# Two turned pairs of attention in one visit of TensorE

## The chip, the cores and the metric

The kernel runs on one core of one Trainium2 chip. The metric is the device time of one execution in microseconds (us); lower is better. An engine is named as in the profile: PE is TensorE, DVE VectorE, ACT ScalarE, POOL GpSimd, SP the queue that issues most DMAs.

## What is computed

A causal attention with a decay over 8 batches and 8 heads (576 positions, 64 channels a head), and on its output a two-layer network with a leaky activation:

```python
scores = scale * np.matmul(q, k.transpose(0, 1, 3, 2))
cum = np.cumsum(np.log(np.clip(f, 0.0001, 1.0)), axis=-1)
scores = np.where(causal, -1000000000.0, scores + cum[:, :, :, None] - cum[:, :, None, :])
attn = np.exp(scores - np.max(scores, axis=-1, keepdims=True))
attn = attn / (np.sum(attn, axis=-1, keepdims=True) + 1e-09)
x = np.matmul(attn, v)              # heads side by side: 4608 tokens x 512
h = x @ w_in                        # 512 -> 2048
g = np.maximum(h, 0.0) + alpha * np.minimum(h, 0.0)
return g @ w_out                    # 2048 -> 512
```

## The kernel before

**Stages.** Two heads make a pair; there are 32 pairs, four to a batch. PE starts on attention, and as soon as the four pairs of a batch have their output, the first layer of the network for that batch can run on it (line 381 with `xx,wi`: 1728 matmuls of 512 columns, twelve to a group that fills one bank of PSUM; the helper `mm` at line 381 issues nearly all matmuls). Attention and first layer share PE until pair 31 is done; then come the rest of the first layer and the second layer (`wot`, `gh`).

**Who sets the order.** The program records operations with a planner (`Plan`), which puts each engine's instructions into a fixed order at build time. It takes on each engine the operation that can begin soonest by its own estimate of durations, and among those the lowest key; a table `SHIFT` adds an offset to the keys by kind of operation and by number. `glue=1.5` lets an operation keep its place at the head though it must wait up to 1.5 us. On the chip each engine then runs its list strictly in order and waits by semaphores.

**A turned pair.** From pair 8 on (`turned`) a pair goes this way:

1. *Tail*: the last 64 queries of both heads, full-array matmuls into two banks (`tail`), small and free to stand anywhere before its pair.
2. *Scores*: twenty matmuls on halves of the rows of the array (64x128 in the profile), two at a time into two banks, six banks in all (`visit`: tiles 0 and 1 share two banks, tile 2 has two, tile 3 has two).
3. DVE reads each bank once (`red`, line 830 for the tiles, 680 for the tail), adds the decay and takes the minimum, and writes into the one buffer `bE`; a bank is free when DVE has read it. ACT takes the exponential in place (line 637).
4. When all nine exponentials are there, DVE turns `bE` in four pieces into four buffers `bm` (line 846, `TK`). `bE` is then free for the next pair.
5. Sixteen DMAs (line 854) gather the pieces into one of two buffers `bTT`: even pairs into the one called `big` in the names, odd pairs into `wr`. Ten are issued by SP, six by POOL.
6. *Values*: sixty matmuls on halves of the columns (128x64) from `bTT` into two banks, which ACT empties (line 925). `bTT` is then free.

So PE meets three layouts of its array: full (first layer, tails), half rows (scores), half columns (values).

**A visit.** `attention(n)` makes one visit for pair n: the values of pair n-2 first, then the scores of pair n. The values carry the requirement that six banks of `rS` are free, and the three groups of scores are glued behind:

```python
after = behind.pop(0) if len(behind) > 1 else None
a = op("PE", ns_v + 400, vp, st, rdy + vd, vb, need=(rS, len(vb[:2]) + 4))
s = op("PE", ..., lambda part=part: rows_of_scores(part), -3000, got, bS[g] + held, glue=1.5)
```

Between two visits stand about four groups of the first layer and one tail. A planned idle time of PE of over half a microsecond in the first 82 us is filled with dummy matmuls (`fill`, line 479), which compute nothing.

Of the kernel before, what the change touches and what calls it, by code (L numbers as in the profile page):

```python
# [18 lines left out]
NP = H // 2  # L19
# [11 lines left out]
NV2 = 6  # L31
# [23 lines left out]
SHIFT = {('L', 0): 9.4, ('D', 0): 2.2, ('Z', 0): 60.6, ('A', 0): 2.2, ('T', 0): -0.3, ('V', 0): -13.3, ('Q', 0): 36.2, ('X', 0): -10.8, ('L', 1): 26.8, ('D', 1): 1.4, ('Z', 1): -27.5, ('A', 1): 47.1, ('T', 1): 17.0, ('V', 1): 48.8, ('X', 1): 122.0, ('L', 2): 28.7, ('D', 2): 45.5, ('Z', 2): 10.6, ('A', 2): 54.0, ('T', 2): 1.8, ('V', 2): 58.1, ('Q', 2): -44.8, ('X', 2): 24.9, ('L', 3): 15.8, ('D', 3): -69.7, ('Z', 3): 0.9, ('A', 3): 165.1, ('T', 3): -84.7, ('Q', 3): 0.7, ('D', 4): -10.7, ('Z', 4): 63.2, ('A', 4): 13.0, ('T', 4): 4.2, ('V', 3): 35.9, ('Q', 4): 132.1, ('X', 3): -15.3, ('L', 5): 81.7, ('D', 5): -4.2, ('Z', 5): -0.4, ('A', 5): 21.2, ('T', 5): -65.7, ('V', 4): 1.3, ('Q', 5): -3.4, ('X', 4): 18.4, ('L', 6): 69.8, ('D', 6): 30.4, ('A', 6): 173.3, ('T', 6): 64.2, ('V', 5): 16.9, ('L', 7): 15.0, ('D', 7): -6.8, ('Z', 7): -95.9, ('A', 7): 218.4, ('T', 7): 47.3, ('V', 6): -17.7, ('V', 7): -37.7, ('Q', 7): -7.0, ('X', 5): -14.8, ('X', 6): -7.2, ('W', 0): 14.3, ('W', 1): 178.8, ('W', 2): 130.1, ('W', 3): -7.0, ('W', 4): 29.0, ('W', 5): 13.1, ('W', 6): 131.9, ('W', 7): -0.1, ('W', 8): -24.7, ('W', 9): 48.7, ('W', 10): -21.0, ('W', 11): -226.7, ('W', 12): -27.8, ('W', 13): 9.3, ('W', 14): 110.8, ('W', 15): 19.8, ('L', 8): -132.0, ('D', 8): -70.2, ('Z', 8): -11.8, ('S', 8): 10.0, ('A', 8): 59.0, ('L', 9): 6.4, ('D', 9): -6.1, ('Z', 9): 32.3, ('S', 9): -81.3, ('A', 9): -1.9, ('Q', 9): -96.4, ('X', 7): 3.1, ('L', 10): 50.1, ('Z', 10): 7.2, ('S', 10): 75.8, ('A', 10): -14.4, ('V', 8): -29.5, ('L', 11): 6.9, ('Z', 11): 41.4, ('S', 11): -6.8, ('A', 11): -68.7, ('V', 9): 12.9, ('Q', 11): 10.9, ('X', 8): 37.3, ('X', 9): 119.6, ('L', 12): 6.3, ('Z', 12): -18.6, ('S', 12): 23.7, ('A', 12): -9.9, ('V', 10): -2.9, ('L', 13): 2.6, ('Z', 13): -3.7, ('S', 13): 27.4, ('A', 13): 27.1, ('V', 11): -0.8, ('Q', 13): -134.7, ('X', 10): 5.7, ('X', 11): 5.8, ('L', 14): 1.6, ('Z', 14): 459.3, ('S', 14): -32.6, ('A', 14): -10.4, ('V', 12): 1.0, ('L', 15): 34.3, ('Z', 15): 17.4, ('S', 15): 96.4, ('A', 15): -40.5, ('V', 13): -69.9, ('Q', 15): -38.3, ('X', 13): 4.3, ('L', 16): 2.7, ('Z', 16): -198.9, ('S', 16): -187.7, ('A', 16): 154.9, ('V', 14): -18.6, ('L', 17): -9.2, ('Z', 17): 0.6, ('S', 17): 49.4, ('A', 17): -109.5, ('Q', 17): -229.2, ('X', 14): 26.2, ('X', 15): -29.2, ('L', 18): -40.0, ('Z', 18): -30.3, ('S', 18): 19.5, ('A', 18): -44.4, ('V', 16): 8.7, ('L', 19): -4.1, ('Z', 19): 16.8, ('S', 19): -29.0, ('A', 19): -99.9, ('V', 17): -19.8, ('Q', 19): -113.9, ('X', 16): 4.8, ('X', 17): -2.5, ('L', 20): -18.2, ('Z', 20): -4.1, ('S', 20): 3.5, ('A', 20): -15.6, ('V', 18): -13.2, ('L', 21): 24.2, ('Z', 21): -5.1, ('S', 21): 30.9, ('A', 21): 1.5, ('V', 19): -12.3, ('Q', 21): -6.5, ('X', 18): -66.7, ('X', 19): 21.5, ('L', 22): -197.2, ('Z', 22): -25.6, ('S', 22): -118.4, ('A', 22): 52.2, ('V', 20): 46.3, ('L', 23): 3.6, ('Z', 23): 49.0, ('S', 23): 3.0, ('A', 23): -4.3, ('V', 21): 106.1, ('Q', 23): -43.7, ('X', 20): 27.7, ('X', 21): -18.4, ('L', 24): -6.9, ('Z', 24): 91.0, ('S', 24): 17.4, ('A', 24): 103.3, ('V', 22): -23.4, ('L', 25): -7.9, ('Z', 25): 14.7, ('S', 25): -51.9, ('A', 25): 20.7, ('V', 23): 21.8, ('Q', 25): 14.2, ('X', 22): 35.9, ('X', 23): -3.3, ('L', 26): -42.8, ('Z', 26): 29.2, ('S', 26): 11.4, ('A', 26): 78.5, ('V', 24): 156.6, ('L', 27): -38.3, ('Z', 27): 1.9, ('S', 27): 40.9, ('A', 27): 0.5, ('Q', 27): 2.0, ('X', 24): -6.8, ('X', 25): 12.5, ('L', 28): -1.5, ('Z', 28): -21.7, ('S', 28): 28.1, ('A', 28): -23.8, ('V', 26): 13.8, ('L', 29): 6.3, ('Z', 29): -5.4, ('S', 29): -109.1, ('A', 29): -4.1, ('V', 27): -32.8, ('Q', 29): -0.6, ('X', 26): -3.0, ('X', 27): -14.3, ('L', 30): -20.4, ('Z', 30): 3.6, ('S', 30): 13.5, ('A', 30): 40.4, ('V', 28): 9.6, ('L', 31): -7.6, ('Z', 31): -99.0, ('S', 31): 13.9, ('A', 31): -1.5, ('V', 29): 16.7, ('V', 31): 16.3, ('V', 30): -2.0, ('Q', 31): -48.0, ('X', 28): -51.3, ('X', 29): -14.3, ('X', 30): -12.2, ('X', 31): -79.3}  # L55
# [167 lines left out]
def attention_moe(  # L223
# [376 lines left out]
    waiting, behind, later_x, quick_ops, value_ops, turn_ops = [], [], [], [], [], []  # L600

    def attention(n):

# [26 lines left out]
        mate = waiting[-1] if n >= NV2 and n % 2 else None  # L630
        bsu = mate[0] if mate else bst
# [132 lines left out]
        def visit(st):  # L764

            plan.at("A", n)
            after = behind.pop(0) if len(behind) > 1 else None
            go = rdy
            if after:
                vb, vp, vd, done = after()  # L770
                a = op("PE", ns_v + 400, vp, st, rdy + vd, vb, need=(rS, len(vb[:2]) + 4))
                value_ops.append(a)
                done(a)
                plan.at("A", n)
                go = [a]
            bS = [[Buf(rS) for _ in range(2)] for _ in range(3)]
            got, where = go, {}
            for g, (tiles, w_) in enumerate((((0, 1), 384), ((2,), 384), ((3,), 512))):
                part = [(i, bS[g], 128 if i == 1 else 0) for i in tiles]
                s = op("PE", (170 if g == 0 else 0) + c_row(w_, nt_), lambda part=part: rows_of_scores(part), -3000, got, bS[g] + held, glue=1.5)  # L780
                got = [s]
                where.update({i: (b_, c0, s) for i, b_, c0 in part})
            s_0.append(s)
            return where

        def stretch(tiles, st):

            plan.at("A", n)
            part = [(i, int(i >= 2 and i != tiles[0]), 128 if i == 1 else 0) for i in tiles]
            bS = [[Buf(rS) for _ in range(2)] for _ in range(1 + part[-1][1])]  # L790
            prods = lambda: rows_of_scores([(i, bS[g], c0) for i, g, c0 in part])

            after = behind.pop() if tiles == (2,) and behind else None
            vb, vp, vd, done = after() if after else ([], lambda: None, [], lambda o: None)
            ns = 340 + sum(c_row(128 * i + 128, nt_) for i in tiles) + (ns_v if after else 0)
            s = op("PE", ns, lambda: (prods(), vp()), st, rdy + vd, [x for y in bS for x in y] + held + vb)
            s_0.append(s)
            if after:
                value_ops.append(s)
            done(s)  # L800
            if n == NE - 1 and tiles[-1] == 3:
                op("-", 0, lambda: setattr(rS, "least", 4), 0, [s])
            return {i: (bS[g], c0, s) for i, g, c0 in part}
# [123 lines left out]
        ns_v = c_m4(256) + 100 + (6 * c_m4(128) + 6 * 112 if turned else 8 * c_m4(128) + 5 * c_m4(64))  # L927
# [24 lines left out]
        bt = None  # L952
        for tiles in ((0, 1), (2,), (3,)) if n < NE else ((2, 3, 0, 1),) if turned else ((0, 1, 3), (2,)):
            where = visit(k0) if turned else stretch(tiles, -61 if n + tiles[0] == 0 else k0 + k_[tiles[0]])
            for i in tiles:
                if i >= 2 and bt is None:
                    bt, nt = tail(k0 + 4)
                bS, c0, s = where[i]
                for h in range(2):
                    tile(h, i, k0 + k_[i] + h, bS[h], s, c0)  # L960

# [9 lines left out]
        behind.append(values)  # L971
        plan.at("V", n)
        if n < NE - 1 or n in (NX[0] - 1, B * NP - 1):
            while behind:
                vb, vp, vd, done = behind.pop(0)()
                value_ops.append(op("PE", ns_v + 250, vp, k0 + 9.6 - hurry, vd, vb))
                done(value_ops[-1])
                plan.at("V", n)
# [11 lines left out]
        elif not (n >= NV2 and n % 2 == 0):  # L990
            keep = 2 if turned else 1
# [98 lines left out]
    for n in range(NX[0], B * NP):  # L1090
        attention(n)

# [301 lines left out]
```

## Time and profile before

| | us |
|---|---|
| median of 3 runs | 990.89 (990.79 to 997.57) |
| the profiled execution | 990.63 |
| its span, first to last instruction | 988.8 |
| PE busy | 982.2 (99%) |
| DVE busy | 830.7 (84%) |
| ACT busy | 614.4 (62%) |
| POOL busy | 375.5 (38%) |

Busy time is the union of an engine's instructions. Matmuls overlap in the pipeline, so PE's busy share says when PE has nothing at all, and not how densely it works; how densely is read from the distance of the starts of successive matmuls.

### The profile page before, as it was taken

To read this page: it belongs to the slowest core of one execution; us is meant where nothing else is said; L and a number is where in the kernel's file an instruction comes from. 1 tells how busy PE (TensorE), PEld (TensorE's weight loads), DVE (VectorE), ACT (ScalarE), POOL (GpSimd) and SP (SyncE) were. 2 spreads that over 40 slices of the span, in tenths; PEclk is the share of its full clock that TensorE was granted. 3 is DMA by queue.
4 is the path that set the end of the run, shared out by engine and by line. 5 is a ranking of instruction groups with operands and counts; after the bars stand their busy time and mean duration, and the time that the engine had idled before them with its cause. 6 is when DMAs were issued, how large, how long until landed. Compare 5 with 4: busy or idle time off the path is not lost.

```text
span 988.8 us, 20133 instructions
## 1 busy us (share of the span) xinstructions
PE 982.2 (99%) x6935; PEld 827.5 (84%) x6935; DVE 830.7 (84%) x1585; ACT 614.4 (62%) x1399; POOL 375.5 (38%) x652
## 2 busy tenths in 40 slices
PE   9999999999999999999999999999999999999998
PEld 5777788888888888888888888999888988898898
DVE  6899988878787778779637988789999999999995
ACT  7888887878677686767635655645444543544352
POOL 5465976888868797777350000000000000000000
PEclk9999999999999999999999999999999999999999
DMA  7977768888888798796757655553444344334521
GB/s 216 260 215 259 251 217 247 254 246 262 247 251 255 224 261 249 219 267 200 215 180 237 203 172 200 174 170 107 149 128 149 107 149 155 122 107 149 169 67 43
DMA packets 133876, 191.68 MB, mean 194 GB/s; under 512 B 22647, under 2 KB 84590, under 8 KB 133774
## 3 DMA queue, kind: packets, MB, share of 16 engines
q1 hardware_dynamic: 128878, 175.73, 57.2%
q0 software_dynamic: 4608, 14.46, 5.3%
q8 instruction: 55, 0.90, 0.4%
q14 instruction: 47, 0.39, 0.1%
q10 hardware_dynamic: 288, 0.20, 0.1%
HBM read 102.95 MB, written 48.67 MB: 153 GB/s over the span
## 4 chain that ended last, share of the span: by engine, by line
PE 96%; DVE 2%; issue 1%; DMA 0%; ACT 0%; DVEq 0%; ACTq 0%
PE bank L381 93%; PE bank L651 2%; PE bank L444 0%; DMA wr<-in_w_in_dram 0%; DVE xs L939 0%; DVE hs L371 0%; DVE big L830 0%; PE bank L729 0%; PE bank L479 0%; DVE hs L1316 0%; DVE big L646 0%; DVE hs L368 0%; DVE wr L371 0%; DVE hs L367 0%; DVE wr L368 0%
## 5 line engine op out<-in xcount | busy, mean ns | idle before, releaser
L381 PE MATMUL bank<-xx,wi 128*128 128x512 f32 x1728 | 407.2, 392 | 0.0
L381 PEld LDWEIGHTS bank<-xx,wi 128*128 128x128 f32 x1728 | 320.4, 188 | 69.6 <-issue 3.0
L637 ACT ACTIVATE big<-big,st 128x384 f32<-128x384 f32 (+4 forms) x272 | 157.7, 582 | 25.8 <-DVE st L830 24.2
L1029 DVE SCALAR_TENSOR_TENSOR hs<-bank,sa,hs 128x512 f32<-128x512 f32 x116 | 86.5, 745 | 54.0 <-ACT hs L1027 52.5
L1027 ACT ACTIVATE hs<-bank,ab 128x512 f32<-128x512 f32 x116 | 79.7, 687 | 70.6 <-PE bank L381 69.0
L830 DVE CUSTOM_DVE_ANT_0 big<-bank,Z 128x384 f32<-128x384 f32 (+1 forms) x220 | 93.0, 480 | 34.2 <-PE bank L381 27.7
L1268 ACT ACTIVATE xx<-gj 128x1792 fp32r<-128x1792 f32 x37 | 62.4, 1701 | 95.0 <-DVE gj L1261 57.3
L381 PE MATMUL bank<-wot,xx 128*128 128x256 f32 (+1 forms) x734 | 120.6, 323 | 0.0
L381 PE MATMUL bank<-wi,xx 128*128 128x256 f32 (+1 forms) x734 | 120.6, 323 | 0.0
L381 PEld LDWEIGHTS bank<-wi,xx 128*128 128x128 f32 x734 | 106.8, 189 | 12.2
L381 PEld LDWEIGHTS bank<-wot,xx 128*128 128x128 f32 x734 | 106.8, 189 | 12.2
L846 DVE STREAM_TRANSPOSE big<-big 128x768 f32<-128x768 f32 x96 | 90.3, 959 | 8.5 <-ACT big L637 8.5
L543 POOL TENSOR_TENSOR Z<-Z,tri 128x128 f32<-128x128 f32 x192 | 79.8, 444 | 34.3 <-DVE Z L513 30.7
L1269 DVE TENSOR_TENSOR xx<-gj,xx 128x1792 fp32r<-128x1792 f32 x37 | 74.4, 2018 | 2.5 <-ACT xx L1268 2.5
L943 POOL TENSOR_TENSOR xx<-xs,xx 128x256 fp32r<-128x256 f32 x64 | 49.0, 781 | 43.2 <-ACT xx L941 42.7
L381 PEld LDWEIGHTS bank<-big,vr 128*64 128x64 f32 x1168 | 53.7, 137 | 9.1 <-issue 5.5
L381 PE MATMUL bank<-wi,gh 128*128 128x256 f32 (+1 forms) x370 | 60.9, 322 | 0.0
L381 PE MATMUL bank<-wot,gh 128*128 128x256 f32 (+1 forms) x370 | 60.9, 322 | 0.0
L381 PE MATMUL bank<-big,vr 128*64 128x128 f32 (+1 forms) x1168 | 59.7, 260 | 0.0
L381 PEld LDWEIGHTS bank<-wot,gh 128*128 128x128 f32 x370 | 53.9, 189 | 6.0
L381 PEld LDWEIGHTS bank<-wi,gh 128*128 128x128 f32 x370 | 53.9, 189 | 6.0
L1298 ACT ACTIVATE hs<-bank 128x256 f32<-128x256 f32 x102 | 36.5, 384 | 24.9 <-PE bank L381 24.6
(164 smaller groups left out, 1585.6 us busy)
## 6 DMA issues: line engine op xcount, KB each, us to landing
hd<-hs SPq DMA_DIRECT2D x144, 256.0 KB
gj<-hd SPq DMA_DIRECT2D x50, 512.0 KB
rqk<-in_qk_dram SPq DMA_DIRECT2D x28, 512.0 KB
wx<-hd SPq DMA_DIRECT2D x22, 512.0 KB
vr<-in_vv_dram SPq DMA_DIRECT2D x32, 320.0 KB
wr<-in_w_in_dram SPq DMA_DIRECT2D x16, 512.0 KB
wx<-in_w_out_dram SPq DMA_DIRECT2D x16, 512.0 KB
out_dram<-hs SPq DMA_DIRECT2D x30, 256.0 KB
```

Of the source, the lines that this page charges most:

```text
L381: pe.matmul(o, lhsT, rhs, start=start, stop=stop)
L543: ms.append(op("POOL", c_po(128), lambda to=to, i=i, zd=zd: po.tensor_tensor(to()[:, :, -1:], zd()[:, :, i : i + 1], tk(), ALU.add), kc + ...
L637: ex = op("ACT", c_exp(w), lambda: ac.activation(at(bt.t), at(bt.t), AF.Exp, bias=lo()[:, col : col + 1], scale=-1.0, accum_out=su()[:, co ...
L651: pe.transpose(t[:, c : c + 128], src[:, 128 * j : 128 * j + 128], ident)
L830: ve.tensor_tensor_reduce(out=o if turned else blk(o), in0=blk(bS.t[:, c0 : c0 + w]), in1=in1(), scale=-0.125, scalar=3.0e38, op0=ALU.add, ...
L846: ve.transpose(part(b_[:, 0 : 768 if k < 3 else MW]), part(bE.t[:, c0 : c0 + (768 if k < 3 else MW)]))
L943: xl = op("POOL", c_po(256), lambda r=r, t0=t0: po.tensor_tensor(bx.t[:, 1, t0 : t0 + 256], bxs[r].t[:, 0:256], bx.t[:, 0, t0 : t0 + 256]. ...
L1027: cp = op("ACT", c_act(512), lambda bh=bh, bs=bs, fc=fc: ac.activation(bs.t, bh.t, AF.Relu, scale=ab[:, fc : fc + 1]), -1000, [last, o_sg] ...
L1029: cp = op("DVE", c_dve(512), lambda bh=bh, bs=bs, fc=fc: ve.scalar_tensor_tensor(bs.t, bh.t, sa[:, fc : fc + 1], bs.t, ALU.mult, ALU.add), ...
L1268: hi = op("ACT", c_acs(896 * GW), lambda w=w, bgh=bgh: ac.activation(bgh.t[:, 0], w(), AF.Copy), key, [o2], [bj, bgh])
L1269: lo = op("DVE", c_dve(896 * GW), lambda w=w, bgh=bgh: tt(bgh.t[:, 1], w(), bgh.t[:, 0].bitcast(F32), ALU.subtract), key + 0.1, [hi], [bj, ...
L1298: side = op("ACT", c_act(256), lambda m=m, slot=slot: ac.activation(bs.t[:, slot], bo[m].t[:, 256:512], AF.Copy), kd, [last], [bo[m], bs])
```

## The change

From pair 10 on, pairs c and c+1 (c even) share one visit. Its order on PE is: scores of c, values of c-3, values of c-2, scores of c+1. `attention` became a generator `steps`, which `couple` drives for two pairs at once. The scores of c ask for five free banks; values and second scores are glued behind them. The normalised output of a pair is finished up to one pair later (`keep = 3`), and the table of offsets is a new one for all pairs, the first eight too.

```diff
-SHIFT = {('L', 0): 9.4, ('D', 0): 2.2, ('Z', 0): 60.6,
+SHIFT = {('L', 0): 51.2, ('D', 0): -3.3, ('Z', 0): -11.8,
...
+    def couple(n):
+        first, second = steps(n, True), steps(n + 1, True)
+        ready = next(first) + next(second)
+        vals = [behind.pop(0) for _ in range(min(2, len(behind) - 1))]
+        for _, d in vals:
+            ready = ready + d()
+        run = [first.send(ready)]
+        for f_, d in vals:
+            vb, vp, vd, done = f_()
+            run.append(op("PE", ns_v[0] + 400, vp, -3000, [run[-1]], vb, glue=1.5))
+            value_ops.append(run[-1])
+            done(run[-1])
+        second.send([run[-1]])
+        for g in (first, second):
+            for _ in g:
+                pass
...
-        def visit(st):
+        def visit(st, go):
             plan.at("A", n)
-            after = behind.pop(0) if len(behind) > 1 else None
-            go = rdy
-            if after:
-                vb, vp, vd, done = after()
-                a = op("PE", ns_v + 400, vp, st, rdy + vd, vb, need=(rS, len(vb[:2]) + 4))
...
-                s = op("PE", (170 if g == 0 else 0) + c_row(w_, nt_), lambda part=part: rows_of_scores(part), -3000, got, bS[g] + held, glue=1.5)
+                s = op("PE", (170 if g == 0 else 0) + c_row(w_, nt_), lambda part=part: rows_of_scores(part), -3000, got, bS[g] + held, glue=1.5,
+                       need=(rS, 5) if g == 0 and n % 2 == 0 else None)
...
+        if turned:
+            go = (yield rdy) if coupled else rdy
+            if n % 2 == 0:
+                bt, nt = tail(k0 - 1)
+            where = visit(k0, go)
+            if coupled:
+                yield s_0[-1]
...
-            keep = 2 if turned else 1
+            keep = 3 if n > NX[0] + 1 else 2 if turned else 1
...
-    for n in range(NX[0], B * NP):
+    for n in range(NX[0], NX[0] + 2):
         attention(n)
+    for n in range(NX[0] + 2, B * NP, 2):
+        couple(n)
```

**PE at the visit of pair 20.** Of before, two first-layer groups (`xx,wi`, with a small transposition between them), then the values of pair 18 (`big`; 14, 10 and 6 rows of two matmuls) and the first scores of pair 20:

```order
L381 MATMUL bank3_79<-xx_88,wi_87 128x512 x12
L729 MATMUL bank1_77<-ident_122,st0_112 18x128
L381 MATMUL bank4_80<-xx_88,wi_87 128x512 x12
L381 MATMUL bank0_76<-big_110,vr_109 64x128 x14
L381 MATMUL bank0_76<-big_110,vr_109 64x64 x10
L381 MATMUL bank6_82<-big_110,vr_109 64x128 x6
L381 MATMUL bank5_81<-Kh0_95,Qh0_93 128x256
L381 MATMUL bank2_78<-Kh0_95,Qh0_93 128x256
```

Of the change, the last scores of pair 20, the values of pairs 17 (`wr`) and 18 (`big`), and the first scores of pair 21:

```order
L381 MATMUL bank7_83<-Kh0_95,Ql0_94 128x512
L381 MATMUL bank4_80<-wr_111,vr_109 64x128 x14
L381 MATMUL bank4_80<-wr_111,vr_109 64x64 x10
L381 MATMUL bank6_82<-wr_111,vr_109 64x128 x6
L381 MATMUL bank2_78<-big_110,vr_109 64x128 x14
L381 MATMUL bank2_78<-big_110,vr_109 64x64 x10
L381 MATMUL bank5_81<-big_110,vr_109 64x128 x6
L381 MATMUL bank1_77<-Kh1_100,Qh1_98 128x256
L381 MATMUL bank0_76<-Kh1_100,Qh1_98 128x256
```

The values stand behind scores now, not behind the first layer, and pair 21's scores follow values, with no first layer between the two pairs.

**SP at the gathering of pair 17.** The rows in which SP comes to the DMAs that fill `wr`; `DMAHW` in the brackets is the queue's own slot. Of before:

```order
L947 DMA xt_62<-xs1_1_118 128x64 [waits DMAHW4_49,Pool_49]
L1031 DMA hd_61<-hs_92 128x512 [waits DMAHW5_49,DVE_49]
L1031 DMA hd_61<-hs_92 128x512 [waits DMAHW6_49,DVE_49]
L854 DMA wr_111<-big_110 32x768 [waits DMAHW7_49,DVE_49]
L854 DMA wr_111<-big_110 32x768 [waits DMAHW0_49]
```

Of the change:

```order
L960 DMA xt_62<-xs1_0_117 128x64 [waits DMAHW5_49]
L1054 DMA hd_61<-hs_92 128x512 [waits DMAHW6_49,DVE_49]
L756 DMA rd2_65<-R1_121 18x128 [waits DMAHW7_49,Activation_49]
L867 DMA wr_111<-big_110 32x768 [waits DMAHW0_49,PE_49]
L867 DMA wr_111<-big_110 32x768 [waits DMAHW1_49]
```

The first DMA of the odd pair waited for DVE, which turns the pair; it now waits for PE, which must have read the values of the pair that lies in `wr`. It is so for ten of the twelve odd pairs from 9 on, and for none on SP before.

**DVE at the turning of pair 18.** Four turns (768, 768, 768 and 800 columns), and behind them the first reads of pair 19's scores. Of before:

```order
L513 STREAM_TRANSPOSE Z0_105<-wr_111 128x2x512
L1029 SCALAR_TENSOR_TENSOR hs_92<-bank1_77,sa_71,hs_92 128x512
L846 STREAM_TRANSPOSE big_110<-big_110 128x768 x2
L1029 SCALAR_TENSOR_TENSOR hs_92<-bank4_80,sa_71,hs_92 128x512
L846 STREAM_TRANSPOSE big_110<-big_110 128x768
L848 STREAM_TRANSPOSE big_110<-big_110 128x32
L846 STREAM_TRANSPOSE big_110<-big_110 128x800
L1029 SCALAR_TENSOR_TENSOR hs_92<-bank6_82,sa_71,hs_92 128x512
L515 STREAM_TRANSPOSE Zt0_106<-sel_127 128x576
L830 ISA big_110,st1_113<-bank2_78,Z1_107 128x4x32
```

Of the change:

```order
L515 STREAM_TRANSPOSE Zt0_106<-sel_127 128x576
L859 STREAM_TRANSPOSE big_110<-big_110 128x768 x2
L1052 SCALAR_TENSOR_TENSOR hs_92<-bank6_82,sa_71,hs_92 128x512
L859 STREAM_TRANSPOSE big_110<-big_110 128x768
L861 STREAM_TRANSPOSE big_110<-big_110 128x32
L859 STREAM_TRANSPOSE big_110<-big_110 128x800
L1052 SCALAR_TENSOR_TENSOR hs_92<-bank7_83,sa_71,hs_92 128x512
L843 ISA big_110,st1_113<-bank3_79,Z1_107 128x4x32
```

The list is nearly the same: turns, with first-layer work (line 1029, in the change 1052) between them, and then the reads of the next pair. What moved is when PE asks for the banks that these reads free: pair 19's scores are already in them.

## Rows read from the trace of the kernel before

**Rows 1.** The page: busy time of all engines, and the chain by engine.
```profile
PE 982.2 (99%) x6935; PEld 827.5 (84%) x6935; DVE 830.7 (84%) x1585; ACT 614.4 (62%) x1399; POOL 375.5 (38%) x652
...
PE 96%; DVE 2%; issue 1%; DMA 0%; ACT 0%; DVEq 0%; ACTq 0%
```
**Rows 2.** Stretches of the span: start:end, length, busy time (instructions) by engine.
```profile
core 0: us, PE busy (x) PEld busy (x) DVE busy (x) ACT busy (x) POOL busy (x), PEclk, DMA share, GB/s
...
40.00:60.00 20.00, 18.71 (x195) 14.28 (x194) 19.26 (x47) 14.69 (x41) 11.72 (x15) 1.00 0.69 220
...
120.00:300.00 180.00, 180.00 (x1491) 149.21 (x1491) 144.60 (x368) 137.80 (x399) 140.88 (x259) 1.00 0.83 248
300.00:480.00 180.00, 180.00 (x1479) 150.09 (x1479) 141.82 (x358) 132.01 (x383) 136.31 (x243) 1.00 0.82 237
```
**Rows 3.** Waits of PE over the whole span: us in total, times, longest.
```profile
PE bank L444 <- DVE wr L441: 1.5, 1, 1.5
PE bank L651 <- ACT big L637: 1.3, 2, 0.9
PE bank L381 <- DVE st L830: 0.5, 1, 0.5
```
**Rows 4.** PE's timeline through one visit: start, length, operation, count.
```profile
309.70 1.77 PE L381 MATMUL bank<-xx,wi 128*128 128x512 f32 x7
311.40 2.99 PE L381 MATMUL bank<-big,vr 128*64 128x128 f32 x60
314.32 0.39 PE L381 MATMUL bank<-Kh,Qh 64*128 64x256 f32 x2
314.54 0.28 PE L381 MATMUL bank<-Kl,Qh 64*128 64x256 f32 x2
314.66 0.28 PE L381 MATMUL bank<-Kh,Ql 64*128 64x256 f32 x2
...
315.98 0.41 PE L381 MATMUL bank<-Kh,Ql 64*128 64x512 f32 x2
316.32 0.38 PE L381 MATMUL bank<-Kh,Qh 128*128 128x256 f32 x1
316.54 0.28 PE L381 MATMUL bank<-Kl,Qh 128*128 128x256 f32 x1
```
**Rows 5.** PE's timeline, an undisturbed run of the first layer.
```profile
513.59 17.75 PE L381 MATMUL bank<-xx,wi 128*128 128x512 f32 x77
```
**Rows 6.** PE's timeline, one stretch of dummy matmuls.
```profile
51.91 1.83 PE L479 MATMUL bank<-ident 128*128 128x128 f32 x14
```
**Rows 7.** All dummy matmuls: duration ns min/median/max, first and last start.
```profile
L479 PE MATMUL bank<-ident x28: 272/275/377, 18.3 to 53.5; 128*128 128x128 f32 x28
```
**Rows 8.** DVE by line and shape: count, busy us, mean ns of one.
```profile
L1029 DVE SCALAR_TENSOR_TENSOR hs<-bank,sa,hs 128x512 f32<-128x512 f32 x116 | 86.5, 745 | 54.0 <-ACT hs L1027 52.5
...
L830 DVE CUSTOM_DVE_ANT_0 big<-bank,Z 128x384 f32<-128x384 f32 x64 | 33.2, 552 | 0.0
L830 DVE CUSTOM_DVE_ANT_0 big<-bank,Z 128x512 f32<-128x512 f32 x48 | 31.2, 685 | 0.5 <-PE bank L381 0.5
...
L846 DVE STREAM_TRANSPOSE big<-big 128x800 f32<-128x800 f32 x24 | 23.5, 978 | 0.0
...
L830 DVE DVE_READ_ACCUMULATOR2_ANT st<- 128x1 f32 x256 | 21.0, 82 | 0.1
L830 DVE CUSTOM_DVE_ANT_0 big<-bank,Z 128x256 f32<-128x256 f32 x48 | 20.1, 419 | 0.0
...
L830 DVE CUSTOM_DVE_ANT_0 big<-bank,Z 128x128 f32<-128x128 f32 x60 | 17.0, 287 | 33.7 <-PE bank L381 27.2 <-POOL Zt L577 2.5 <-POOL Z L557 1.8
```
**Rows 9.** The sixteen gathering DMAs of a pair (line 854): issue in ns min/median/max, landing.
```profile
L854 SPq DMA_DIRECT2D big<-big x120: 507/588/1471, 141.5 to 492.4; - x120
L854 SPq DMA_DIRECT2D wr<-big x120: 507/582/1904, 154.5 to 502.4; - x120
...
DMA to landing us min/median/max: 2.1/4.0/6.0
```

More of the change, by code (lines that the diff above doesn't have):

```diff
@@ L598, in load_n, with steps @@
         return out, rz, rt, bZ, [(lambda a, b, q=q: q()[:, a - 128 : b - 128], k) for q, k in ((Qh, Kh), (Qh, Kl), (Ql, Kh))] + [(lambda a, b: q0(), k0_)]
-    waiting, behind, later_x, quick_ops, value_ops, turn_ops = [], [], [], [], [], []
+    waiting, behind, later_x, quick_ops, value_ops, turn_ops, ns_v = [], [], [], [], [], [], []
     def attention(n):
+        for _ in steps(n):
+            pass
[14 more added lines that the diff above has]
+            for _ in g:
+                pass
+    def steps(n, coupled=False):
         b, p = divmod(n, NP)
@@ L628, in attention @@
         bxs = [Buf(rxs[r]) for r in range(2)]
-        mate = waiting[-1] if n >= NV2 and n % 2 else None
-        bsu = mate[0] if mate else bst
+        mate, bsu = None, bst
         lo, su = (lambda: bst.t[:, 0:10]), (lambda: bsu.t[:, 19:28] if mate else bsu.t[:, 10:19])
@@ L762, in rows_of_scores @@
                         mm(o, q(128 * i, 128 * i + 128)[r], kk, c == 0, c == len(some) - 1)
-        def visit(st):
+        def visit(st, go):
             plan.at("A", n)
-            after = behind.pop(0) if len(behind) > 1 else None
-            go = rdy
-            if after:
-                vb, vp, vd, done = after()
-                a = op("PE", ns_v + 400, vp, st, rdy + vd, vb, need=(rS, len(vb[:2]) + 4))
[L772 to L775, printed above, removed]
             bS = [[Buf(rS) for _ in range(2)] for _ in range(3)]
@@ L793, in stretch @@
             after = behind.pop() if tiles == (2,) and behind else None
-            vb, vp, vd, done = after() if after else ([], lambda: None, [], lambda o: None)
-            ns = 340 + sum(c_row(128 * i + 128, nt_) for i in tiles) + (ns_v if after else 0)
+            vb, vp, vd, done = after[0]() if after else ([], lambda: None, [], lambda o: None)
+            ns = 340 + sum(c_row(128 * i + 128, nt_) for i in tiles) + (ns_v[0] if after else 0)
             s = op("PE", ns, lambda: (prods(), vp()), st, rdy + vd, [x for y in bS for x in y] + held + vb)
@@ L925, in copy_v @@
             xs_ops[r].append(op("ACT", c_act(w_), lambda: ac.activation(bxs[r].t, bP.t[:, 0:w_], AF.Copy), st, [pvo], [bP, bxs[r]]))
-        ns_v = c_m4(256) + 100 + (6 * c_m4(128) + 6 * 112 if turned else 8 * c_m4(128) + 5 * c_m4(64))
+        ns_v[:] = [c_m4(256) + 100 + (6 * c_m4(128) + 6 * 112 if turned else 8 * c_m4(128) + 5 * c_m4(64))]
         v_deps = lambda: ([] if turned else e1) + e2[0] + e2[1] + e3 + [e4, o_zero] + l_v
@@ L951, in attention @@
         k_ = (0, 2, 6, 8) if n < NE else (0, 0.5, 2, 3) if turned else (0, 2, 8, 6)
-        bt = None
+        bt = where = None
+        if turned:
[5 more added lines that the diff above has]
+                yield s_0[-1]
+        mate = waiting[-1] if n >= NV2 and n % 2 else None
+        bsu = mate[0] if mate else bst
         for tiles in ((0, 1), (2,), (3,)) if n < NE else ((2, 3, 0, 1),) if turned else ((0, 1, 3), (2,)):
-            where = visit(k0) if turned else stretch(tiles, -61 if n + tiles[0] == 0 else k0 + k_[tiles[0]])
+            where = where or stretch(tiles, -61 if n + tiles[0] == 0 else k0 + k_[tiles[0]])
             for i in tiles:
@@ L960, in attention @@
                     tile(h, i, k0 + k_[i] + h, bS[h], s, c0)
+            where = None
         def done_v(r, bP):
@@ L969, in values @@
                     lambda o: [done_v(r, bP[r])(o) for r in (1, 0)])
-        behind.append(values)
+        behind.append((values, v_deps))
         plan.at("V", n)
@@ L974, in attention @@
             while behind:
-                vb, vp, vd, done = behind.pop(0)()
-                value_ops.append(op("PE", ns_v + 250, vp, k0 + 9.6 - hurry, vd, vb))
+                vb, vp, vd, done = behind.pop(0)[0]()
+                value_ops.append(op("PE", ns_v[0] + 250, vp, k0 + 9.6 - hurry, vd, vb))
                 done(value_ops[-1])
```

2 lines of the change are left out of this document (1 added, 1 removed).

## The prediction

> **What bounds the kernel now.** First the page: PE is busy 99% of the span, and 96% of the chain that ended last is PE [rows 1]. Then the stretches: from 120 to 480 us PE is busy 360 of 360 us, while DVE has 80%, ACT 75%, POOL 77% and the DMA engines 82 to 83% [rows 2]. The waits of PE come to 3.3 us in the whole span [rows 3]. The only gap of note is at the start: from 40 to 60 us PE works 18.71 of 20, and DVE, at 19.26, is what it follows there [rows 2]. So in the part that the change rewrites there is no wait to remove; only how densely PE works can change, and that is read from the distance of starts. Undisturbed, 77 first-layer matmuls take 17.75 us, 0.23 each [rows 5]. One visit shows where that pace is lost [rows 4]: where the layout of the array changes.
>
> **What a change of layout costs.** Full to values: seven full matmuls take 309.70 to 311.40, 1.70 where 7 × 0.23 is 1.61: 0.09 lost ahead of the first values. What the first values lose is inside a merged row; if it is as much as their neighbours lose, the change costs 0.2, if nothing 0.1; I take 0.15. Values to scores: the first two scores take 314.32 to 314.54, 0.22, the next two 0.12: 0.10 lost, and as much again unseen ahead of them by the pattern of the next change. Scores to full: 315.98 to 316.32 is 0.34 instead of 0.23, and 316.32 to 316.54 is 0.22 instead of 0.12: 0.21. So a change costs about 0.2 us on entering scores or full, 0.15 on entering values. [rows 4] The Trainium skill (TensorEngine Tiling (Array Packing), section Key Properties) says that switching the tiling mode, and not just the tile, drains TensorE. It has no figure; the 0.2 us of rows 4 agrees with it.
>
> **What the change removes.** Counting the layouts in the two instruction orders from the first turned scores on, I find 78 changes before and 63 after. Entries to scores go from 26 to 27, to full from 28 to 22, to values from 24 to 14: values now come behind scores or behind other values, and the two pairs of a visit share its ends. That is 5 × 0.2 + 10 × 0.15 = **2.5 us** off PE (bounds 15 × 0.1 = 1.5 and 15 × 0.2 = 3.0). At the start, changed only by the table, changes go from 63 to 60, which I count at nothing (at most 0.6).
>
> The dummy matmuls go from 28 records to 18 by the order. One stretch has 14 in 1.83 us, whose last lasts 0.27 [rows 6, 7], so (1.83 − 0.27) / 13 = 0.12 each, and ten are 1.2 us. They fill time that the planner thought idle. If that time is really gone, PE gains **1.2**; if PE then waits instead, nothing. I take 1.2, as the planner puts fewer of them only where it found less idle time. The gap of the start I keep: DVE, whose work is the same, sets the pace from 40 to 60 us; at most the 1.3 us that PE idles there vanish or double [rows 2].
>
> Otherwise the work is the same: matmuls by shape, and operations of DVE, ACT, POOL and SP, apart from one load's target. The last part of PE's order, from the last values on, is the same too.
>
> **What it adds: a wait for `wr`.** The values of c−3, c even, used to be read well before pair c−1 was gathered into the same buffer; SP's DMA waited for the turning alone. Now they stand inside the visit, and c−1 can be gathered only behind them. From the end of the values of c−3 the chain is: ten DMA issues of SP at 0.58, 5.8 us (POOL issues its six beside them); landing, 4.0 at the median, 2.1 to 6.0 [rows 9]; then the four buffers of turned pieces are free and the last piece of pair c can be turned, 0.98; with that `bE` is free; a first-layer operation of DVE may stand between, 0.75; then DVE reads the first two banks of pair c+1, 0.29 + 0.08 + 0.42 + 0.08 = 0.87 [rows 8]. Together 12.4 us (10.5 to 14.4 with the landing).
>
> Meanwhile PE has the values of c−2 (311.40 to 314.32, 2.92) and the scores of c+1 (314.32 to 316.32, 2.00), 4.9 us [rows 4]. So the first bank of c+1 comes free 12.4 − 4.9 = 7.5 us after its scores end (5.6 to 9.5). What PE has to do before it writes into such a bank I counted from the order, a first-layer matmul at 0.23 [rows 5]: it is 30 or 42 of them, with or without a tail, and for the ten couples 12, 14, ... 30 it comes to 7.9, 7.55, 9.5, 7.2, 9.5, 9.9, 6.8, 9.5, 6.8 and 9.9 us. PE waits where 7.5 is more: 0.3 at pair 18, 0.7 each at 24 and 28, **1.7 us** in all. With landings of 2.1 nothing waits; with 6.0 the waits are 1.6 + 2.0 + 2.3 + 2.7 + 2.7 = 11.3. I take the median, as the issues are spread over 5.8 us, and a slow landing of an early one is not the last to end. Behind the waiting turn on DVE stand first-layer reads (lines 1029 and 1052), which free PE's other two banks; behind the waiting DMA on SP stand the stores of `hd`, for which nobody waits soon.
>
> **The sum** is made against the profiled execution, 990.63, 0.26 below the median of the runs. 990.6 − 2.5 − 1.2 + 1.7 = **988.6 us**.
>
> **Rivals.**
>
> *B, the wait is covered everywhere.* If SP's ten issues start early, or landings are nearer to 2.1 than to 4.0 [rows 9], no couple waits: 990.6 − 2.5 − 1.2 = 986.9, and with switches at their upper bound (0.5), the start's gap gone (1.3) and its three switches (0.6) 984.5. For it: the DMA engines have 17% free [rows 2], and five couples of ten have 2 us to spare at the median. Against it: three have none, and the landings meet the other DMAs.
>
> *C, the wait decides (slower).* If the last of the sixteen DMAs sets the chain and lands as late as the slowest of before, 6.0, the ten couples lose 11.3: 990.6 − 3.7 + 11.3 = 998.2. It cancels the gain at a landing of 4.5 (7.5 + 0.5 = 8.0 us: 0.1 + 0.45 + 0.8 + 1.2 + 1.2 = 3.75 lost), half a microsecond above the median: that is close. For it: sixteen landings and not one must be in, and the DMA engines are 83% busy. Against it: five couples have 9.5 us or more and lose only above 6.0; to be over 1% slower, 9.9 us, the loss must be 13.6, which takes 6.3 us at all ten, longer than any of before.
>
> *D, the gain comes back at the banks within a visit.* Scores of c take six banks and values of c−3 two, but only five need be free when the visit begins. The first group's banks are read about 2.00/3 + 0.87, some 1.5 us, after the scores begin, and the scores last 2.0 [rows 4, 8], so it is hidden, unless DVE holds a first-layer operation of 0.75 just then: up to 0.4 us at each of nine visits, 3.6, and the time is 990.6 − 2.5 − 1.2 + 1.7 + 3.6 = 992.2. DVE has 20% free [rows 2], so it isn't late as a rule. The Trainium skill (the same page, section Performance Considerations, PSUM Bottleneck) warns that tiling speeds up TensorE but not the emptying of PSUM, and that the copy out may become the bottleneck; this is the rule that speaks against putting two pairs' scores into one visit. In rows 8, one pair's eight reads of banks are 2 × (0.29 + 0.42 + 0.55 + 0.69) and eight times 0.08, some 4.5 us, against 2.0 us of scores, which agrees with the rule; by it alone D would be the likeliest and 992 the time. What speaks against it here is that 5.8 us of values stand between the two scores.
>
> **How the numbers follow.** My forecast, most couples covered and a few short waits, 0.47; B 0.27; C 0.17; D 0.09. The likeliest has 988.6, by its own bounds 987 to 991 (0.5 and 1.0 for the switches, 1.2 for the dummies, 1.7 either way for the new waits, not all at once). The range goes from 985.0 (B to its lower end, with 0.03 left out below) to 995.0 (all of D, and half of C, 0.1 left out above). One per cent is 9.9 us, about what a measurement of this kernel tells from no change. Faster by that would need more than half as much again as B's lower end gives (6.1): 0.01. Slower by that is C with landings above 6.3: 0.06. Within it: 0.93.
>
> **What would show it.** For each step: as many first matmuls of scores with a start 0.22 after them as the order has entries, and fewer full ones; 18 dummy records; PE busy 360 of 360 us from 120 to 480; or, where C or D holds, waits of PE from 150 us on that end with DVE's reads of scores, ahead of first-layer matmuls for C and ahead of values for D; SP's gathering DMA for `wr` waiting for PE and the turning on DVE waiting for a DMA. The forecast is wrong if PE waits for over 4 us there, if the start's waits change by over 2 us, or if the time of a change of layout depends on what follows.

## The result, and the profile after

The changed kernel takes 1000.01 us at the median of 5 runs (998.65 to 1000.89), the kernel before 991.11 in the same series: a ratio of 1.0086, with a 95% interval of 1.0067 to 1.0105. It is slower by 8.9 us between the medians, where the prediction had 988.6 and a range to 995.0. The profiled execution took 1000.89, of which the span is 999.0 (988.8 before).

The page of the profile after, against [rows 1]: engines, and the chain that ended last.

```profile
PE 983.0 (98%) x6925; PEld 826.6 (83%) x6925; DVE 827.7 (83%) x1585; ACT 610.4 (61%) x1399; POOL 372.0 (37%) x652
...
PE 85%; DVE 5%; DMA 4%; SPq 3%; issue 1%; ACT 0%; DVEq 0%; ACTq 0%
```

PE's share of the chain went from 96% to 85%; DVE, the DMAs and SP's queue stand in it now. The stretches that answer to [rows 2], and the waits of PE that answer to [rows 3] (us in total, times, longest):

```profile
120.00:300.00 180.00, 174.57 (x1395) 143.33 (x1391) 144.86 (x362) 129.82 (x382) 138.99 (x252) 1.00 0.79 229
300.00:480.00 180.00, 177.02 (x1411) 146.92 (x1411) 137.10 (x339) 125.56 (x364) 131.59 (x235) 1.00 0.81 233
```

```profile
PE bank L381 <- DVE hs L1052: 6.1, 6, 1.6
PE bank L381 <- DVE st L843: 2.1, 3, 0.9
PE bank L444 <- DVE wr L441: 1.5, 1, 1.5
```

From 120 to 480 us PE is busy 351.6 of 360 us; before it was all 360. What it waits for is DVE, above all line 1052, the first layer's read of a bank, and hardly the reads of scores (line 843; one of its three waits is at 68 us). From 160 to 480 us all six waits of PE end with line 1052, each behind a turning; the four from 120 to 160 us, 2.1 in all, end with other operations of DVE. On DVE the turning waits for the gathering DMAs of the odd pairs, 21 times, and SP's first DMA into that buffer waits for PE:

```profile
DVE big L859 <- DMA wr<-big: 61.4, 21, 6.3
```

```profile
SPq L867 <- PE bank L381: 35.2, 10, 4.4
```

**One couple.** The chain of waits through couple 16, from the end of the values of pair 13 (start, length, what):

```profile
244.84 5.86 PE bank L381 x86
...
250.71 0.54 SPq L867
251.25 0.05 issue
251.30 0.58 SPq L867
251.88 0.05 issue
251.94 0.58 SPq L867
...
252.56 1.26 SPq L867
...
254.59 0.72 SPq L638
...
257.47 0.60 SPq L867
258.07 0.04 issue
258.11 4.94 DMA wr<-big
...
263.24 0.17 DVE big L861
263.41 0.65 DVE hs L1052
264.05 0.04 issue
264.10 3.03 PE bank L381 x12
```

The chain is the one that the prediction laid out, up to its last link. SP's first nine gathering issues take from 250.71 to 258.07, 7.4 us where the prediction had 5.8 for all ten (the tenth ends at 258.70), since some issues are slow and a load of `vr` (line 638) stands among them; the landing takes 4.94. DVE in the same stretch:

```profile
257.20 0.98 DVE L859 STREAM_TRANSPOSE big<-big 128x768 f32<-128x768 f32 x1 [5.34 <-DMA wr<-big]
258.11 0.71 DVE L1052 SCALAR_TENSOR_TENSOR hs<-bank,sa,hs 128x512 f32<-128x512 f32 x1
259.31 0.98 DVE L859 STREAM_TRANSPOSE big<-big 128x768 f32<-128x768 f32 x1 [0.49 <-DMA wr<-big]
262.34 0.98 DVE L859 STREAM_TRANSPOSE big<-big 128x768 f32<-128x768 f32 x1 [2.05 <-DMA wr<-big]
263.24 0.17 DVE L861 STREAM_TRANSPOSE big<-big 128x32 f32<-128x32 f32 x1
263.33 0.71 DVE L1052 SCALAR_TENSOR_TENSOR hs<-bank,sa,hs 128x512 f32<-128x512 f32 x1
263.96 1.00 DVE L859 STREAM_TRANSPOSE big<-big 128x800 f32<-128x800 f32 x1
```

And PE, whose first-layer work stops at 262.35, after thirty matmuls:

```profile
250.50 2.94 PE L381 MATMUL bank<-big,vr 128*64 128x128 f32 x60
...
255.37 7.14 PE L381 MATMUL bank<-xx,wi 128*128 128x512 f32 x30
264.10 2.11 PE L381 MATMUL bank<-xx,wi 128*128 128x512 f32 x8 [1.59 <-DVE hs L1052]
```

The read that would free PE's next bank is the one at 263.33, behind a turning that waits for a DMA until 262.34. Scores of the next pair hold six banks in this time, so the first layer has two, and both go through DVE's list.

**A second place.** Pair 9's scores are read late as well. Ahead of them DVE splits the last of the first layer's weights (line 372):

```profile
135.38 4.29 DVE L372 SCALAR_TENSOR_TENSOR wr<-wi,wr 128x512 f32<-128x512 f32 x1
```

This operation took 0.69 to 1.85 us elsewhere in this profile. POOL, meanwhile:

```profile
135.41 1.30 POOL L595 TENSOR_TENSOR Ql<-rqk,Qh 128x512 fp32r<-128x512 f32 x1
136.64 1.01 POOL L867 DMA_DIRECT2D big<-big  x2
137.67 1.44 POOL L595 TENSOR_TENSOR Kl<-rqk,Kh 128x576 fp32r<-128x576 f32 x1
```

**The account.** It is made from distances of starts, since short waits hide in PE's busy time. Up to the first turned scores the new kernel is 0.5 us behind (124.01 us with 126 first-layer matmuls done, against 130.36 with 156; thirty are 6.8 us). From 139 to 155 us five distances are 3.3 us too long together. From 160 us to the end of attention such excesses make 7.4 us: 0.6 at couple 12, 1.3 at 14, 1.75 at 16, 1.5 each at 22 and 24, 0.8 at 28. Behind seven waits the next distance is about 0.1 longer too, in the first layer 0.34 instead of 0.23 (0.8 us). The changes of layout give 2.5 back, by their count and the distances read at them. That is 0.5 + 3.3 + 7.4 + 0.8 − 2.5 = 9.5 of the 10.2 us between the spans; 0.7 are not assigned.

### The profile page after: what moved, and what is told of

Read it like the earlier page. It is cut to its first block, busy times and chain, and to the rows that moved or that the text cites. A ratio compares the mean times of both kernels' runs of the same rounds, so it can differ in the third digit from the quotient of the medians.

```text
span 999.0 us, 20048 instructions
## 1 busy us (share of the span) xinstructions
PE 983.0 (98%) x6925; PEld 826.6 (83%) x6925; DVE 827.7 (83%) x1585; ACT 610.4 (61%) x1399; POOL 372.0 (37%) x652
## 4 chain that ended last, share of the span: by engine, by line
PE 85%; DVE 5%; DMA 4%; SPq 3%; issue 1%; ACT 0%; DVEq 0%; ACTq 0%
PE bank L381 83%; SPq L867 3%; DMA wr<-big 3%; PE bank L672 1%; DVE big L843 1%; DVE big L859 1%; DMA wr<-in_w_in_dram 1%; DMA Zt<-c 1%; DVE wr L372 1%; DMA rqk<-in_qk_dram 0%; PE bank L444 0%; DVE xs L952 0%; DVE hs L1052 0%; DVE wr L371 0%; DVE wr L368 0%
## 5 line engine op out<-in xcount | busy, mean ns | idle before, releaser
L859 DVE STREAM_TRANSPOSE big<-big 128x768 f32<-128x768 f32 x96 | 91.2, 967 | 63.7 <-DMA wr<-big 61.4
```

What stands on the lines that cost most here:

```text
L859: ve.transpose(part(b_[:, 0 : 768 if k < 3 else MW]), part(bE.t[:, c0 : c0 + (768 if k < 3 else MW)]))
```

## The experiments

Each edit is to the changed kernel, unless it says otherwise. The edits are shown in part: code that holds an operation back until another has been issued is left out, and comments are added. W and T are the two theories: the loss comes from the wait for the odd pairs' buffer, or from the order that the new table makes. "PE idle" is PE's time without work from 160 to 530 us, read from the stretches of each profile (6.2 us in the changed kernel, nothing before); single waits of PE are shorter there than the excesses above by what is still in the pipeline.

### The wait taken away

```diff
+            src = lambda: rTT.store.items[0] if n % 2 and n >= 9 else bTT.t
-            tt_of = lambda x, a0=0, a1=4: bTT.t.rearrange(...)
+            tt_of = lambda x, a0=0, a1=4: src().rearrange(...)
```

> Edit to the changed kernel: the values of the odd pairs from 9 on read the buffer of the even pairs, so their product is that of other data; nobody reads the odd pairs' buffer then, and the gathering DMAs into it need not wait for the values of pair c-3. The instructions of every engine stand in the same order. Theory W (the values inside the visit delay the gathering, DVE's turning waits for it, and the first-layer reads of banks behind it on DVE keep PE waiting): DVE's waits for these DMAs go from 61.4 us to under 10, PE's gaps after 160 us from 7.4 us to under 1, each gap with 0.1 of restart, so about 992 (991 to 993.5). Theory T (the order made by the new table costs the time): unchanged, 999 to 1001.

Measured: 995.11 us (993.55 to 996.60), outside both ranges. DVE's waits for these DMAs went from 61.4 to 13.6 us and no couple waited, but a wait came that was not there before: the values of pair 29 stand outside a couple and had to wait for the gathering of pair 30. PE's timeline there, and the stretches around it (PEclk is the third number from the end):

```profile
491.04 1.55 PE L381 MATMUL bank<-xx,wi 128*128 128x512 f32 x6
494.90 4.63 PE L381 MATMUL bank<-big,vr 128*64 128x128 f32 x60 [2.31 <-DMA big<-big]
499.46 3.06 PE L381 MATMUL bank<-xx,wi 128*128 128x512 f32 x12
502.44 2.99 PE L381 MATMUL bank<-big,vr 128*64 128x128 f32 x60
```

```profile
492.00:496.00 4.00, 1.69 (x15) 1.29 (x15) 2.05 (x8) 3.25 (x11) 2.78 (x4) 0.88 0.76 223
496.00:500.00 4.00, 4.00 (x54) 3.77 (x51) 0.00 (x0) 0.81 (x3) 0.00 (x0) 0.69 0.38 117
500.00:504.00 4.00, 4.00 (x39) 3.25 (x39) 2.11 (x4) 2.77 (x8) 0.82 (x2) 1.00 0.44 131
```

PE idled 2.31 us, and then the clock granted was 0.88 and 0.69 over two stretches of 4 us, a mean of the full 2.4 GHz and of the lower level of 1.2; the sixty matmuls of these values took 4.63 us, those of the next pair 2.99. So in the profiled run the edit's own wait cost 2.3 + 1.6 = 3.9. The same run with pairs 29 and 31 left as they were (`n % 2 and n < 29`):

> As the first run without the wait, but only the odd pairs whose values stand in a shared visit (9 to 27) read the even pairs' buffer (so their product is that of other data); pairs 29 and 31 are as in the changed kernel, since in the first run the values of 29 had to wait 2.3 us for the gathering of pair 30, a wait that the edit itself had made. Theory W: the 7.4 us of PE's gaps after 160 us and 0.1 of restart behind each go, and no new one comes: 991 to 992.5. If the wait costs only what the first run showed (1000 to 995.1), 994.5 to 995.5.

Measured: 992.08 us (991.30 to 992.71, 10 runs), ratio to before 1.0015 (1.0006 to 1.0024). PE is idle nothing from 160 to 530 us; from 120 us on its waits were those of pairs 9 and 10 alone, two of them among the three of this line (the third is in the start):

```profile
PE bank L381 <- DVE st L844: 2.2, 3, 0.9
```

All instructions stood in the same order, with the same table, so the loss that went, 8 us between the medians and 7 by the two ratios, belongs to the wait. (The edit also spares the odd pairs' values the wait for their own gathering, but no such wait of PE stands in the profile of the changed kernel.) What is left, 1.5 us over the kernel before, doesn't belong to it; the account above has 0.5 + 3.3 − 2.5 = 1.3 for it.

### The wait made longer

```diff
+        both = []
         for f_, d in vals:                                    # values c-3, then c-2
             vb, vp, vd, done = f_()
+            if len(vals) == 2:
+                both.insert(0, vp)                            # both issued at the second place, c-2 first
+                vp = (lambda: None) if len(both) == 1 else lambda: [x() for x in both]
             run.append(op("PE", ns_v[0] + 400, vp, -3000, [run[-1]], vb, glue=1.5))
```

> Edit to the changed kernel: inside a visit the values of c-2 stand ahead of those of c-3, all else in the same order, so the buffer of the odd pairs comes free 2.9 us later. Theory W: the six couples at which PE already waits lose 2.9 us each, the other four between 0 and 2.9: 17 to 29 us more, 1017 to 1029. Theory T: within 1 us of 1000.

Measured: 1033.88 us (1031.02 to 1036.75), 34 us more, above the range. PE idle is 28.0 us. Its waits: 15.6 us for first-layer reads, 7.2 for the scores' reads, and 7.1 for a reason that the expectation lacked, the first values of a visit waiting eight times for ACT to empty their banks (line 942). From 330 to 390 us the granted clock is 0.94, not 1.00. So W's direction and order of size hold, its number does not: the edit also moved a wait of another kind.

### First-layer reads ahead of the turning, all of them

On DVE a turning was held until the reads (line 1052) right behind it had been issued, as far as the turning's own DMAs allowed, so reads moved ahead by one or two places.

```diff
+            if o.tag == "turn":
+                self.hold.append(o)      # issued before any other DVE operation or a DMA that needs it
+            else:
+                o.fn()
```

> Edit to the changed kernel: on DVE, first-layer reads of banks (line 1052) that stood behind a turning move ahead of it, one or two places, as far as the DMAs behind the turning allow; the other engines' lists are the same. If PE waits because first-layer reads are queued on DVE behind the waiting turning (theory W in its last link), at least half of the 6.1 us that PE waits for line 1052 goes: 994 to 997. If PE waits for the banks of the scores of c+1, as the prediction had it, nothing is gained: 999 to 1001.

Measured: 1025.34 us (1023.26 to 1027.40), 25 us slower. Neither theory had foreseen that.

```profile
PE bank L387 <- DVE st L849: 7.3, 9, 2.0
PE bank L387 <- DVE st L707: 7.1, 9, 1.9
PE bank L387 <- DVE hs L1059: 2.6, 6, 1.1
```

```profile
DVE hs L1059 <- ACT hs L1057: 94.2, 58, 6.5
DVE big L865 <- DMA wr<-big: 35.8, 12, 6.3
```

PE's wait for first-layer reads did fall from 6.1 to 2.6 us, but DVE now waits 94.2 us (42.0 before the edit) for ACT, that is for reads whose bank was not full yet, with turnings and then the scores' reads behind them, and PE waits 14.4 us for those (lines 849 and 707). An engine that runs its list in order pays for either order where it is wrong.

### One read at the place that waits

In six even pairs (from 12 on) the third turning lets the one read behind it pass.

```diff
+                        if k == 2 and n % 2 == 0 and n >= 12:
+                            tn.tag = "turn"
```

> Edit to the changed kernel: in six even pairs the first-layer read that stands on DVE right behind the third turning moves ahead of it; all else in the same order. If that place is where PE's waits of couples 16, 22, 24 and 28 come from (1.75, 1.5, 1.5 and 0.8 us), up to 5.5 us go: 994.5 to 997. If the read isn't ready by then, the turning and all behind it are late instead, as in the run with all reads ahead, and it is 1000 or more.

Measured: 997.17 us (996.79 to 998.66), 2.8 us faster than the changed kernel between the medians (2.1 by the ratios), 0.2 above the range that was expected if that place is the cause. Couple 16 no longer waits: its read stands at 259.17 and PE runs 42 first-layer matmuls in one go there.

```profile
259.17 0.75 DVE L1064 SCALAR_TENSOR_TENSOR hs<-bank,sa,hs 128x512 f32<-128x512 f32 x1 [1.11 <-ACT hs L1062]
259.83 0.97 DVE L869 STREAM_TRANSPOSE big<-big 128x768 f32<-128x768 f32 x1
```

```profile
253.99 9.86 PE L391 MATMUL bank<-xx,wi 128*128 128x512 f32 x42
```

PE's waits for first-layer reads fell from 6.1 to 0.9 us; 1.1 us came back at reads of scores and 1.0 at POOL.

### The reads left out

```diff
-                cp = op("DVE", c_dve(512), lambda ...: ve.scalar_tensor_tensor(bs.t, bh.t, sa[...], bs.t, ...), ...)
+                cp = op("DVE", c_dve(512), lambda: None, ...)
```

> Edit to the changed kernel: the first layer's operation on DVE (line 1052, its negative half) is left out while attention runs, so a bank is free when ACT has read it; all else in the same order, and the wait for the odd pairs' buffer stays. If PE waits through first-layer reads queued on DVE behind the waiting turning, DVE still waits over 45 us for the DMAs but PE's gaps after 160 us fall from 7.4 to under 2 us: 992 to 994.5. If it waits for the banks of the scores of c+1, as the prediction's count had it, gaps stay where little work covers them (couples 18, 24, 28) and the time is 996 or more.

Measured: 995.88 us (994.55 to 998.89); PE idle falls from 6.2 to 1.1 us while DVE's turning waits as long as ever:

```profile
DVE big L859 <- DMA wr<-big: 67.2, 26, 6.3
```

So the turning's wait reaches PE through the first layer's reads behind it on DVE, and hardly by the scores' banks: with the reads gone, PE idles 1.1 us beside 67.2 us of waiting on DVE, and 0.6 of that is a wait for POOL. The time is 1.4 us above the expected range; DVE is also freed of 86 us of work by this edit, so it says which path the wait takes, and less what the path costs.

### SP's issue shortened

```diff
+                            if n % 2 and n >= 11 and j % 8 == 2:
+                                q_ = po              # 8 of 16 gathering DMAs of an odd pair on POOL, 6 before
```

> Edit to the changed kernel: of the sixteen gathering DMAs of the odd pairs from 11 on, POOL issues eight instead of six and SP eight instead of ten; all else in the same order. Theory W (the pace of issue is part of the chain that DVE's turning waits for): SP's part gets 2 x 0.58 = 1.2 us shorter, so each of the six waits of PE loses up to 1.2: 5 to 6.5 us, 993.5 to 995. If the last landing counts and not the issue, 999 to 1001.

Measured: 1000.09 us (999.20 to 1002.74), no gain. In its profile PE idle is 4.5 instead of 6.2 us: couple 16's wait is gone, a new one of 1.0 us has come at couple 20, and the others are between 0.2 longer and 0.6 shorter, not 1.2 shorter. Eight issues of SP still took from 250.85 to 257.44 in couple 16, with the load of `vr` among them. In the ten couples SP's part takes 5.5 to 7.2 us where ten issues took 6.6 to 8.0, and yet the last turning starts 9.3 to 12.6 us after the end of the values of pair c-3, 11.2 at the median, as in the changed kernel (9.0 to 13.3, median 11.2). So shortening SP's part did not bring the turning forward; whether the landings or POOL's two more issues hold it stays open.

### POOL's order at pair 10

Two gathering DMAs of pair 8 are issued by POOL ahead of its line 595 instead of behind it.

```diff
+                if n == 10 and hi is Qh:
+                    out[-1].tag = "later"       # issued when POOL's next operation that is no gathering comes
```

> Edit to the changed kernel: two of POOL's gathering DMAs of pair 8 move ahead of the split of pair 10's queries (line 595); all else in the same order. In the changed kernel the last split of the first layer's weights on DVE (line 372) starts at 135.38 within 0.03 us of POOL's work on line 595 and lasts 4.29 us instead of 0.7 to 1.9, and pair 9's reads behind it are late. If POOL's arithmetic holds DVE's operation, the operation now ends before POOL's begins, takes under 2 us, and PE's gaps from 139 to 155 us (3.3 us in all) shrink: 996.5 to 998.5. If it isn't POOL's arithmetic, 999 to 1001.

The split on DVE now lies beside POOL's issues alone:

```profile
136.08 0.69 DVE L379 SCALAR_TENSOR_TENSOR wr<-wi,wr 128x512 f32<-128x512 f32 x1
```

It takes 0.69 us instead of 4.29, so it was POOL's arithmetic that held it. The Trainium skill (SBUF — State Buffer, section SBUF: two separate sides) says that VectorE and GpSimd share a pair of ports to SBUF as an exclusive lock, for a VectorE operation with two inputs in SBUF too, against a GpSimd operation that reads SBUF; the 4.29 and 0.69 us agree in kind. Why the operation ended only at 139.67, 0.6 us behind POOL's second operation and 3 us behind its first, no run here shows. The waits at 139 and 150 us went, those between pair 10's scores stayed, and PE's idle time from 130 to 160 fell from 2.2 to 0.8 us. The time did not fall: 1000.35 us (997.25 to 1002.93), where 996.5 to 998.5 was expected. In the profiled run attention was 1.6 us shorter and the start 0.7 longer, and some couples' waits were longer (2.3 instead of 1.7 at one distance). Among runs that lie 5.7 us apart, 1.5 us can't be told.

### Both taken away

The run without the wait, plus POOL's order:

> The second run without the wait for the odd pairs' buffer (same replaced operand in the values of pairs 9 to 27) and, on top, POOL's order of the third edit (line 372 on DVE not held by line 595). If these two are what turned the gain into a loss, what is left is the saving of the changes of layout against the start: 992.1 less the 1.1 us (gaps of 1.25 and 0.8 turned into plain distances, less what came back at 151 us) to 3.3 us of the gaps from 139 to 155: 989 to 991, at the kernel before's 990.5 or under it. Otherwise it stays at 992.

Measured: 991.66 us (989.78 to 995.49, 10 runs), ratio 1.0018 (1.0004 to 1.0033); above the expected 989 to 991 and not clearly below the run without the wait alone (992.08, ratio 1.0015). The profiled run, one of the faster ones, has a span of 989.0 where before has 988.8. So with both obstacles gone the couples come within 2 us of the kernel before, and don't pass it: in the profile about 1.5 of the 2.5 us that they should save go at the scores of pair 10, which still wait for DVE from 150 to 154 us, and 0.6 at the start. Neither here nor in the run before does the time show what POOL's order is worth.

### Table and structure apart

The kernel before with the new table:

> The kernel before with the new table of offsets, and no couples. Theory W: the table by itself moves little, 989 to 994, and no wait of DVE's turning for the gathering DMAs. Theory T: the loss is the table's, 996 or more.

Measured: 1009.23 us (1008.22 to 1010.29), in T's range and not in W's. The turning waited for gatherings 2.7 us in all; on PE one wait of 6.5 us stands out, of the first layer for its input from POOL (line 943), and the granted clock was 0.77 from 150 to 180 us, the stretch around it. The changed kernel with the old table:

> The changed kernel with the table of offsets of the kernel before. Theory W: the couples wait for the odd pairs' buffer all the same, so DVE's turning waits for these DMAs by tens of us and the kernel is slower than before, 997 or more. Theory T: the table is what costs, and with the old one the couples bring their 2.5 us: 986 to 990.

Measured: 1021.44 us (1017.43 to 1022.06), in W's range. DVE's turning waits 45.0 us for the gatherings here too, and there are waits for first-layer input that neither kernel has. Last, a planner that knows of later landings:

```diff
-                end = self.chan + 1.0
+                end = self.chan + 1.0 + o.late       # 1.5 for the gathering DMAs
```

> Edit to the changed kernel: the planner takes the gathering DMAs to land 1.5 us later than it did, so that it knows of the wait and orders all engines anew (67 changes of layout for 63). Theory W: DVE's wait for these DMAs falls below 40 us and PE's waits for line 1052 below 3 us; the time is 993 to 1000 where the new order costs nothing elsewhere. Theory T (any order that the table wasn't made for costs): over 1003.

Measured: 1004.44 us (1004.13 to 1004.75). DVE's wait fell to 32.5 us and PE's waits for first-layer reads to 2.2 (1.9 of it at one tail), as W has it, and yet the time is in T's range: its new order has other waits, 3.6 and 1.8 us behind the end of attention, and 67 changes of layout. The three orders that the planner made anew are 4 to 21 us slower than the kernels they were made from, so what they bear out is T as the last expectation has it, that an order costs which the table wasn't made for. T as the claim that the new table is bad in itself can't be tried this way: each table is bad under the other structure. The runs above this section, which keep the order or change named places of it, are the ones that tell causes apart.

## Why the prediction was wrong

**What held.** The terms without the wait did: a change of layout costs what was read. After, a scores' entry behind first layer is 0.32 and 0.22 where plain distances are 0.23 and 0.12, the first distance into values 0.154 beside 0.103, and the count was 63, so by count and distances 2.5 us came; no run shows them by themselves. The dummies went to 18 records, but the start as a whole was 0.5 us later, so the 1.2 did not come. The landing's median was 4.0 us in both kernels, as assumed, and the chain from the values to the turning exists link by link, with SP waiting for PE at ten odd pairs.

**The step that failed** is the cover: "What PE has to do before it writes into such a bank I counted from the order". The count ran to the first write into a bank of pair c+1's scores, 42 matmuls or 9.5 us in couple 16. PE stopped after 30, at the third first-layer group, since the bank of an earlier group was still to be read by line 1052, behind the turning. The prediction names these reads as standing behind the waiting turning, and gives them no price. That took 2.7 us of cover from couple 16 and as much from 22, which the count had among the safest. Up to the bank that PE lacked the cover of couple 16 is 250.69 to 262.35, 11.7 us, and the chain to the end of the read that frees it, 250.69 to 264.05, took 13.4.

A second term was mis-sized with it, the chain. From the end of the values to the start of the last turning the sum had 5.8 + 4.0 = 9.8 us; in the ten couples it was 9.0 to 13.3, median 11.2, and 13.3 in couple 16. SP's ten issues took 6.6 to 8.0 us for 5.8; the landing of couple 16 took 4.9 for 4.0. Couple 18, which the count had as waiting, had the shortest chain, 9.0, and did not wait. In couple 16 it took both errors: at the forecast's sizes that read would have ended about 5.8 + 4.0 + 1.0 = 10.8 us after the values (an estimate, with the 1.0 from landing to read of the chain above), inside the cover of 11.7; and with the reads left out, waits as long of DVE left PE 1.1 us idle in all. So the forecast's 1.7 us became 7.4, and 0.8 of restarts behind them that no term had.

**What it lacked altogether** is the place at pair 9, 3.3 us. The sum took the start's and the table's effects as nothing, since the work is the same; but the new order put DVE's two-input operation beside POOL's, and made it 4.29 us. These 3.3 us are read from distances in one profile; no run's time shows them.

**The rivals.** C, the wait that decides, was right in sign and in the buffer, and wrong in its condition and its banks: it asked for landings of over 4.5 us and for waits that end with the reads of scores; the loss came at the usual landings (median 4.0, as before) and at first-layer reads. D is not what happened: no value waited for a bank from 160 us on, in the changed kernel. The Trainium skill's warning (TensorEngine Tiling (Array Packing), section Performance Considerations) that PSUM's emptying may become the bottleneck agrees only in part: PE waited 6.1 us for first-layer banks, with six of unread scores held beside them, but because DVE, which empties them, was waiting for DMAs.

## What to carry to other kernels

When a change makes an engine wait, list everything behind the waiting instruction on that engine and ask for each when its reader needs it; the first of these to be needed sets the cover, not the buffer that the wait is about. Cover counted in "work until the buffer is needed again" must stop at the first bank whose release stands in the same list. To find causes in a planned kernel, change one operand or swap one pair of instructions in the finished order; a planner that runs anew moves more than the cause is worth.

## What the runs showed of the hardware

Idle time of PE can cost more than itself. In the first run without the wait a wait of 2.31 us was followed by a granted clock of 0.69 over 4 us, and values that took 4.63 us for 2.99; in the changed kernel, whose single waits of PE from 120 us on are up to 1.6 us, the clock stayed at 1.00. Several short waits close together went otherwise: in the kernel before with the new table, PE waited 0.40, 0.20 and 0.58 us between 151 and 155 us, and the granted clock was 0.68 from 154 to 158 us. Even a short wait is followed by a first-layer distance of 0.34 us for 0.23, as behind the 1.6 us of couple 16. And a two-input operation of VectorE that starts with POOL's arithmetic took 4.29 us for 0.69, past two operations of POOL and the DMA issues between them.
